# In-place weight decoding, a zero-padded first unit, a second block by halves and backward priorities in a linear-attention and gated-MLP kernel

## The chip, the cores and the metric

The kernel runs on one core of one Trainium2 chip. A core has TensorE (PE: matmuls, with its weight loads shown apart as PEld), VectorE (DVE), ScalarE (ACT), GpSimd (POOL) and SyncE (SP), which here issues nearly all DMAs. SBUF is the on-chip memory of 128 partitions; PSUM holds the results of matmuls in eight banks. The metric is the device time of one execution in microseconds (us). Lower is better.

## The reference

Two stages follow each other. The first is a recurrent attention with a decaying state, the second a two-layer MLP with a gate that is 0 below -1, a parabola between -1 and 1, and the identity above 1.

```python
B, H, S, D = 4, 8, 768, 48                 # batch, heads, tokens, head size
state = zeros(B, H, D, D)
for t in range(S):
    cur = einsum('bhd,bhe->bhde', u * k[t], v[t])
    y[t] = einsum('bhd,bhde->bhe', r[t], state + cur)
    state = w[t][..., None] * state + einsum('bhd,bhe->bhde', k[t], v[t])
x = y.transpose(0, 2, 1, 3).reshape(3072, 384)
h = x @ w_in                               # 384 -> 2048
g = where(h >= 1, h, where(h <= -1, 0, (h + 1)**2 / 4))
out = g @ w_out                            # 2048 -> 384
```

All of it is float32. The kernel gets float32 accuracy from the faster 32-bit matmul format (fp32r in the profile) by splitting each operand into a high and a low part and adding three products.

## The kernel before

**Units and blocks.** The 3072 tokens are cut into 12 units of 256 (three units to a batch). Function `attention(u, ...)` works on one unit: running products of w by scans on VectorE (p forward, y backward), k divided and r multiplied by them (lines 400 and 450), the matrix of r and k inside each chunk of 64 tokens on TensorE (`among`, line 420), masked into r_ by predicated copies (line 426), k transposed (line 459) and copied to SBUF (kt, line 466), the update of the state for each chunk (`umat`, line 481), a chain of four states on VectorE (lines 497 to 500: add the old state, multiply by the decay), and the output: state times r (`cross` and a part of `along`) and r_ times v (`along`, line 519). The first three units are "early": they get k times u on ScalarE (line 390) and a second `among`; the others use the natural layout nk.

**From y to x.** A unit's eight heads of 48 stand in four slots of two heads, 64 rows each, with 48 used. The MLP wants 384 rows in three groups of 128. So three slots keep their place, and the fourth slot (tile last) is cut in pieces of 16 rows, which six DMAs (line 603, function `fill`) move into the free rows 48 to 63 of x. Before that, x and last are written as high and low part (`yevac`, lines 571 to 575): ScalarE copies the high part from PSUM, VectorE subtracts it for the low part. For a unit in INPLACE (unit 0), TensorE subtracts the high part in PSUM (`less`, lines 581 and 584) and ScalarE copies the rest.

**MLP steps.** Two units make a block of 512 tokens; there are six blocks. A step (b, f) of `products` takes block b and one of the 16 slices f of 128 hidden units: nine matmuls into h (line 849), the gate (lines 665 to 670: two on ScalarE, one on VectorE, a high-part copy on ScalarE, a low part on VectorE), and, LAG steps later, nine matmuls that add into three PSUM banks acc (line 869). In block 0 the first five f are taken by halves, 256 tokens each: half 0 needs only unit 0, half 1 only unit 1.

**Weights.** Each slice f of the weights comes as 64-bit words (768 KB) and is decoded once by `weight(f)`: fetch into wraw; ScalarE writes the exponent and mantissa part to fl (line 320) and 16 low bits to rr (line 323), GpSimd 16 sign bits to rr (line 324), VectorE shifts and merges fl and rr (line 327), ScalarE copies the high part (line 316), VectorE subtracts for the low part (line 330). There are two fl tiles, one rr tile, and at most FLIGHT = 4 fetches at a time.

**Order of the work.** The program lists its operations with an engine, a cost, what they read and write, and a due time. A planner (class Plan) orders them before anything runs: at each moment it gives each engine the ready operation with the smallest key, where a key is the time of a step minus a lead (LEADS for each unit, DECODE for weights, SLACK times the length of what follows in the group). It repeats this ROUNDS = 6 times with the step times of the last round and keeps the order whose modelled end is first. Every engine then runs its own list strictly in this order, so an instruction that waits holds up all behind it on its engine. Where TensorE would be idle, matmuls on zeros are inserted (lines 292 and 298), which compute nothing.

## Time and profile before

| | |
|---|---|
| median of 3 runs | 526.85 us (526.12 to 532.59) |
| the profiled execution's own time | 525.53 us |
| its span, first to last instruction | 523.8 us |
| mean granted TensorE clock | 0.998 |
| matmuls (line 849, line 869) | 909 and 909 |

Times in the profile count from the first instruction of the span. A timeline row gives start, duration, engine, line, operation, output and input; where equal instructions follow each other they are merged into one row, and xN is their count. Brackets hold the idle time of the engine just before and what ended it. A row of the groups gives line, engine, operation, shape and count, then busy time in us and the mean in ns of one, then the idle time before them. A row of stages gives the stage, its length, and the busy time and number of instructions of PE, PEld, DVE, ACT and POOL, then the granted clock, the busy share of the DMA engines and GB/s. Matmuls overlap in a pipeline, so a pace is read from two starts, not from a duration.

### The profile page before, as it was taken

Reading aid. Unit: us, or ns where it says so; the run is one execution under the profiler, and the core shown is the slowest. Engines: PE = TensorE matmul, PEld = TensorE weight load, DVE = VectorE, ACT = ScalarE, POOL = GpSimd, SP = SyncE. Lnnn points to the kernel's source line nnn. Section 1 sums busy time; section 2 is a strip of 40 time slices with the busy share of each in tenths; the row PEclk is TensorE's granted clock in tenths of the full one; section 3 lists DMA queues with packets and bytes.
Section 4 is the critical chain, followed back from the end, with each engine's and each line's share of the span. In section 5 each row is a group of like instructions: output and inputs, shape, how many; then the busy total and the mean of one; then the engine's idle time right before and its main releaser. Section 6 shows DMA issues by size and latency. Waiting matters only on the chain.

```text
span 523.8 us, 12249 instructions
## 1 busy us (share of the span) xinstructions
PE 501.5 (96%) x5168; PEld 398.2 (76%) x5168; DVE 339.7 (65%) x575; ACT 293.0 (56%) x573; POOL 94.8 (18%) x61
## 2 busy tenths in 40 slices
PE   7879899999999999999999999999999999999994
PEld 5457887777887787787788687887788777788883
DVE  7999999899955889785692443965833545333331
ACT  5677888677784555653462544634644344444442
POOL 3564744550220311101110001101000100000000
PEclk9999999999999999999999999999999999999999
DMA  8985932525650624530330101504100100100001
GB/s 323 408 281 164 354 107 76 190 91 174 199 172 3 208 96 134 195 102 14 120 109 1 62 0 32 176 2 128 61 0 0 43 18 10 68 1 0 1 0 66
DMA packets 22190, 54.83 MB, mean 105 GB/s; under 512 B 3184, under 2 KB 9072, under 8 KB 22128
## 3 DMA queue, kind: packets, MB, share of 16 engines
q1 hardware_dynamic: 21840, 53.59, 29.8%
q8 instruction: 42, 0.69, 0.5%
q10 hardware_dynamic: 288, 0.39, 0.2%
q14 instruction: 20, 0.16, 0.1%
HBM read 46.89 MB, written 4.72 MB: 99 GB/s over the span
## 4 chain that ended last, share of the span: by engine, by line
PE 74%; DVE 11%; issue 4%; DMA 4%; POOL 3%; SPq 1%; ACT 1%; ACTq 0%; DVEq 0%; POOLq 0%
PE h L849 33%; PE acc L869 32%; PE bank L519 3%; POOL rr L324 3%; DMA rk<-in_rk 2%; PE bank L481 2%; PE bank L420 2%; PE bank L459 2%; DVE fl L327 1%; DVE g L667 1%; DMA wraw<-in_wbits 1%; DVE wt L330 1%; DVE p L377 1%; DVE gl L670 1%; DVE rk L450 1%
## 5 line engine op out<-in xcount | busy, mean ns | idle before, releaser
L849 PE MATMUL h<-x,wt 128*128 128x512 f32 (+1 forms) x909 | 221.0, 389 | 4.7 <-DVE g L667 3.3
L849 PEld LDWEIGHTS h<-x,wt 128*128 128x128 f32 x909 | 162.9, 188 | 43.9 <-DVE g L667 6.3
L869 PE MATMUL acc<-gh,wt 128*128 128x512 f32 (+1 forms) x606 | 154.7, 390 | 0.0
L667 DVE SCALAR_TENSOR_TENSOR g<-g,h 128x512 f32<-128x512 f32 (+1 forms) x101 | 65.7, 655 | 98.5 <-ACT g L666 98.4
L869 PEld LDWEIGHTS acc<-gh,wt 128*128 128x128 f32 x606 | 108.6, 188 | 24.4 <-issue 0.5
L665 ACT ACTIVATE g<-h 128x512 f32<-128x512 f32 (+1 forms) x101 | 57.9, 574 | 103.9 <-PE h L849 99.9
L670 DVE TENSOR_TENSOR gl<-g,gh 128x512 fp32r<-128x512 f32 (+1 forms) x101 | 68.9, 686 | 31.6 <-ACT gh L669 31.3
L669 ACT CAST gh<-g 128x512 fp32r<-128x512 f32 (+1 forms) x101 | 60.0, 597 | 46.8 <-DVE g L667 45.9
L869 PE MATMUL acc<-gl,wt 128*128 128x512 f32 (+1 forms) x303 | 84.1, 385 | 0.8 <-DVE gl L670 0.8
L869 PEld LDWEIGHTS acc<-gl,wt 128*128 128x128 f32 x303 | 55.6, 188 | 13.7 <-DVE gl L670 1.1
L666 ACT ACTIVATE g<-g 128x512 f32<-128x512 f32 (+1 forms) x101 | 61.6, 611 | 2.6
L324 POOL TENSOR_SCALAR rr<-wraw 128x768 uint16<-128x768 uint16 x16 | 55.0, 3435 | 44.6 <-DVE fl L327 23.9
L446 POOL TENSOR_TENSOR r<-cst,d 128x512 f32<-128x512 f32 x18 | 20.3, 1146 | 215.2 <-PE bank L519 184.7
L377 DVE TENSOR_TENSOR_SCAN p<-wq,seeds 128x520 f32<-128x520 f32 x24 | 30.5, 1272 | 2.9 <-DMA wq<-in_w 2.0
L372 DVE TENSOR_TENSOR_SCAN y<-wq,seeds 128x520 f32<-128x520 f32 x24 | 31.5, 1311 | 0.8
L438 POOL TENSOR_TENSOR nk<-nk 128x768 f32<-128x768 f32 x9 | 17.3, 1926 | 63.8 <-DMA nk<-in_nk 39.3
L499 DVE TENSOR_TENSOR sm<-bank,st 128x192 f32<-128x192 f32 x39 | 13.9, 356 | 10.8 <-PE bank L481 8.9
L320 ACT ACTIVATE fl<-wraw 128x768 f32<-128x768 f32 x16 | 14.5, 915 | 8.6 <-DVE wt L330 8.6
L519 PEld LDWEIGHTS bank<-rk,st 64*64 64x64 f32 x656 | 12.3, 134 | 8.6 <-issue 3.3
L400 DVE TENSOR_TENSOR rk<-rk,y 128x512 f32<-128x512 f32 x24 | 17.1, 712 | 2.3 <-DMA rk<-in_rk 2.1
L426 DVE COPY_PREDICATED r<-below,bank 128x512 f32<-128x512 int32 x22 | 15.6, 731 | 4.5 <-PE bank L420 3.6
L323 ACT ACTIVATE rr<-wraw 128x768 uint16<-128x768 uint32 x16 | 17.4, 1084 | 0.9 <-DMA wraw<-in_wbits 0.9
(89 smaller groups left out, 386.6 us busy)
## 6 DMA issues: line engine op xcount, KB each, us to landing
rk<-in_rk SPq DMA_DIRECT2D x24, 512.0 KB, 5.1
wraw<-in_wbits SPq DMA_DIRECT2D x16, 768.0 KB, 7.5
nk<-in_nk SPq DMA_DIRECT2D x9, 768.0 KB, 4.6
wq<-in_w SPq DMA_DIRECT2D x24, 260.5 KB, 3.0
vn<-in_v SPq DMA_DIRECT2D x12, 384.0 KB, 6.2
fl<-in_w SPq DMA_DIRECT2D x12, 260.0 KB, 3.2
out_y<-g SPq DMA_DIRECT2D x10, 256.0 KB, 2.4
x<-last SPq DMA_DIRECT2D x72, 32.0 KB, 3.1
```

The costliest lines, as they stand in the source:

```text
L324: op(SIGNS, 0.6 if SIGNS == "DVE" else 1.3, due, [("raw", f)], ["rr_high"], lambda: (V if SIGNS == "DVE" else G).tensor_scalar(out=r16[:, ...
L372: V.tensor_tensor_scan(out=y_[:, ::-1], data0=w[:, SEG:0:-1], data1=sv[:, ::-1], initial=0.0, op0=ALU.mult, op1=ALU.add)
L377: V.tensor_tensor_scan(out=pv[:, q].rearrange("p n c -> p (n c)"), data0=w[:, 0:SEG], data1=sv, initial=0.0, op0=ALU.mult, op1=ALU.add,)
L446: op("POOL", 1.1, due, ["d", "cst"], [("R", h)], lambda h=h: G.tensor_tensor(out=r_[h], in0=twice.unsqueeze(1).unsqueeze(1).broadcast_to([ ...
L519: PE.matmul(out=bank[by[g]][HP * half : HP * half + HP, lo : lo + C], start=first, stop=False, skip_group_check=True, **kw)
L665: op("ACT", c, due, [("b", 6 + hk)], [("g", gk)], lambda: nc.scalar.activation(gs, hs, AF.Relu, scale=0.5, bias=0.5))
L666: op("ACT", c, due, (), [("g", gk)], lambda: nc.scalar.activation(gs, gs, AF.Square))
L667: op("DVE", 0.13 + 0.53 * k, due, [("b", 6 + hk)], [("g", gk)], lambda: nc.vector.scalar_tensor_tensor(out=gs, in0=gs, scalar=1.0, in1=hs, ...
L669: op("ACT", c, due, [("g", gk)], [("gh", gk)], lambda: nc.scalar.copy(ghs, gs))
L670: op("DVE", 0.15 + 0.5 * k, due, [("g", gk), ("gh", gk)], [("gl", gk)], lambda: nc.vector.tensor_tensor(out=gls, in0=gs, in1=ghs.bitcast(F ...
L849: nc.tensor.matmul(hp, lhsT=wx[f][:, cs], rhs=xt[:, j, :], start=n == 0, stop=n == 8)
L869: nc.tensor.matmul(o[j], lhsT=wx[f][:, cs], rhs=gt, start=first and i == 0, stop=stop and i == 2, skip_group_check=True)
```

## The change

Seven things change together.

1. **Weights in place.** The three pieces of the decoding that come before the merge are written back into wraw itself, so rr is gone and fl only takes the merged result; there are three fl tiles (FULL), and FLIGHT goes from 4 to 3. GpSimd now takes the sign from the 32-bit high word after ScalarE's piece, not from 16-bit words beside it; the three pieces follow one another. The merge reads two operands with a step of two words.
2. **Unit 0 padded** (ALONE). Its v comes from a second layout, v0, with 64 columns a head of which 16 are zero, and its states stand in padded tiles (borrowed from ob and g). So rows 48 to 63 of the first three slots of y are zero; the fourth slot is copied (last_f) and added into these rows by six float32 matmuls with a permutation matrix perm (`spread`). The six fill DMAs of unit 0 are gone. Two DMAs for v0 and one for perm take the place of one for v; there are two more memsets on GpSimd.
3. **Unit 0's chain of states** (CHAINED): the old state is added on TensorE, into the PSUM bank that holds the update (`add_up`), and VectorE only multiplies.
4. **Unit 1 joins INPLACE.** Its low parts come from TensorE and ScalarE.
5. **Block 1 by halves** for its first 14 f (HALVES).
6. **k times u on VectorE, the copies to ptot on GpSimd**; the last output's DMA of acc bank 1 is issued from SP, not from ACT. APART = 1 concerns the fills of unit 0 alone, of which there are none.
7. **Priorities.** One round with due times (ROUNDS = 1, new LEADS, SLACK and DECODE), then five rounds (BACK) in which the keys come from a schedule made backwards from the end (`late`); the best of the six is kept.

```diff
-HALVES = 5
+HALVES = {0: 5, 1: 14}
+BACK = 5
@@ Plan.best, after the rounds with due times
+        for _ in range(BACK):
+            for op, key in zip(self.ops, self.late()):
+                op["key"] = key
+            order = self.order()
+            end = max(self.end.values())
+            if end < found[0]:
+                found = end, order, (self.begin, self.end)
+    def late(self):
...
+        while any(open_.values()):
+            t, e = min((max(free.get(e, 0.0), min(ready(n) for n in ns)), e) for e, ns in open_.items() if ns)
+            n = max((n for n in open_[e] if ready(n) <= t + 1e-9), key=lambda n: (self.end[n], n))
...
+            back[n] = free[e] = t + ops[n]["cost"]
...
+        return [last - back[n] for n in range(len(ops))]
@@ parameters
-LEADS = {0: 33.0, 1: 17.9, 2: 36.0, 3: 22.6, 4: 34.7, 5: 44.0, 6: 70.6, 7: 38.2, 8: 38.8, 9: 10.1, 10: 28.0, 11: 37.9}
-LEAD, DECODE = 15, 11.9
-FLIGHT = 4
+LEADS = {0: 81.9, 1: 72.9, 2: 33.1, 3: 18.5, 4: 28.8, 5: 10.1, 6: 29.8, 7: 19.1, 8: 36.5, 9: -4.7, 10: 28.9, 11: -2.7}
+LEAD, DECODE = 15, 9.3
+FLIGHT = 3
+FULL = 3
-SIGNS = "POOL"
-INPLACE = {0}
+ALONE = {0}
+INPLACE = {0, 1}
+CHAINED = {0}
-ROUNDS = 6
+ROUNDS = 1
@@ weight
-        op("ACT", 0.9, due, [("raw", f)], [("fl", k)], lambda: A.activation(
-            s, wraw[f][:, :, 1].bitcast(F32), AF.Abs, scale=float(2.0**-112)))
-        op("ACT", 1.07, due, [("raw", f), ("flight", f % FLIGHT)], ["rr_low"],
-           lambda: A.activation(r16[:, :, 0], wraw[f][:, :, 0].bitcast(U32), AF.Copy, scale=LOW))
-        op(SIGNS, 0.6 if SIGNS == "DVE" else 1.3, due, [("raw", f)], ["rr_high"], lambda: (V if SIGNS == "DVE" else G).tensor_scalar(
-            out=r16[:, :, 1], in0=wraw[f].rearrange("p c two -> p (c two)").bitcast(U16)[:, 3::4],
-            scalar1=32768.0, scalar2=32768.0, op0=ALU.is_ge, op1=ALU.mult), port=SIGNS == "DVE")
-        op("DVE", 0.95, due, ["rr_low", "rr_high"], [("fl", k)], lambda: V.scalar_tensor_tensor(
-            out=m, in0=m, scalar=3, in1=rr, op0=ALU.logical_shift_left, op1=ALU.bitwise_or), port=True)
+        op("ACT", 0.9, due, (), [("raw", f)], lambda: A.activation(high(F32), high(F32), AF.Copy, scale=float(2.0**-112)))
+        op("ACT", 1.07, due, (), [("raw", f)], lambda: A.activation(half(0), low(U32), AF.Copy, scale=LOW))
+        op(on, 0.62 if f in SIGNS else 3.15, due, (), [("raw", f)], lambda: e.tensor_scalar(
+            out=half(1), in0=high(F32), scalar1=0.0, scalar2=32768.0, op0=ALU.is_lt, op1=ALU.mult))
+        op("DVE", 0.95, due, [("raw", f), ("flight", f % FLIGHT)], [("fl", k)], lambda: V.scalar_tensor_tensor(
+            out=s.bitcast(I32), in0=high(), scalar=3, in1=low(), op0=ALU.logical_shift_left, op1=ALU.bitwise_or), port=True)
@@ attention
+        if alone:
+            for c2 in range(2):
+                load(due, g_[c2], a["v0"][c2], [("g", c2)])
+            load(due, perm, a["perm"], ["perm", "nk"])
-                A.mul(ku[:, q, cs], rk[slot[q]][:, 1, cs], u_col[:, 2 * q + pr : 2 * q + pr + 1])
+                V.tensor_scalar(
+                    out=ku[:, q, cs], in0=rk[slot[q]][:, 1, cs], scalar1=u_col[:, 2 * q + pr : 2 * q + pr + 1],
+                    scalar2=None, op0=ALU.mult)
-            op("ACT", 0.2, due, [("p", q)], [("ptot", u, q)], lambda q=q: A.copy(
+            op("POOL", 0.2, due, [("p", q)], [("ptot", u, q)], lambda q=q: G.tensor_copy(
+        def add_up(c, old):
+            c2, g = divmod(c, 2)
+            PE.matmul(bank[bu[g]][:, c2 * 4 * D : (c2 + 1) * 4 * D].rearrange("p (a e) -> p a e", e=D), lhsT=ident, rhs=ss_(old),
+                      start=False, stop=True, skip_group_check=True)
+        def spread(g):
+            yv = bank[by[g]].rearrange("p (a c t) -> p a c t", a=4, t=C)
+            for j in range(3):
+                PE.matmul(yv[:, j], lhsT=perm[:, 128 * j : 128 * j + 128], start=False, stop=True, skip_group_check=True,
+                          rhs=last_f.rearrange("p (c g t) -> p c g t", c=2, g=2)[:, :, g, :])
+        if alone:
+            for g in range(2):
+                op("ACT", 0.27, due, [("b", by[g])], [("last_f", g), ("g", 2)], lambda g=g: A.copy(
+                    last_f.rearrange("p (c g t) -> p c g t", c=2, g=2)[:, :, g, :],
+                    bank[by[g]].rearrange("p (a c t) -> p a c t", a=4, t=C)[:, 3]))
+            for g in range(2):
+                op("PE", 0.65, due, [("last_f", g), "perm", "nk", ("g", 2)], [("b", by[g])], lambda g=g: spread(g), fresh=False)
-        for j in range(3):
+        for j in range(0 if alone else 3):
@@ products, the last step
-            out("ACT", nc.scalar, "ACT", 1, whole)
+            out("ACT", nc.sync, "SP", 1, whole)
```

147 lines of the change are left out of this document (106 added, 41 removed).

## The prediction

> **What bounds the kernel now.** I read the page first: which engine fills the span.
>
> ```profile
> span 523.8 us, 12249 instructions
> PE 501.5 (96%) x5168; PEld 398.2 (76%) x5168; DVE 339.7 (65%) x575; ACT 293.0 (56%) x573; POOL 94.8 (18%) x61
> ```
>
> TensorE does. But its 96% is an average that also counts matmuls on zeros, so next I cut the span at TensorE's own landmarks: first MLP product, first product of half 1, first full step all paid up, start of block 1.
>
> ```profile
> 0.00:33.43 33.43, 24.81 (x488) 16.68 (x489) 28.87 (x44) 19.39 (x40) 17.37 (x22) 1.00 0.91 342
> 33.43:52.21 18.78, 17.55 (x348) 15.17 (x347) 17.58 (x35) 15.95 (x35) 9.96 (x3) 1.00 0.61 210
> 52.21:68.51 16.30, 14.75 (x114) 13.94 (x113) 15.84 (x26) 14.56 (x29) 12.45 (x5) 1.00 0.80 302
> 68.51:122.42 53.91, 52.17 (x681) 40.60 (x680) 50.22 (x83) 40.32 (x73) 24.14 (x10) 1.00 0.37 124
> 122.42:170.00 47.58, 47.58 (x417) 37.97 (x420) 33.67 (x56) 33.66 (x72) 6.72 (x4) 1.00 0.41 132
> 170.00:516.97 346.97, 344.61 (x3141) 273.88 (x3132) 193.07 (x335) 168.31 (x328) 24.16 (x19) 1.00 0.18 60
> ```
>
> The columns after the stage's length are PE, PEld, DVE, ACT, POOL busy, clock, DMA share, GB/s. From 68.51 on TensorE is idle for 1.74, 0 and 2.36 us only: nothing that VectorE, ScalarE or GpSimd save there can be seen, unless TensorE's own work changes. Before 68.51 VectorE is the full engine (17.58 of 18.78, 15.84 of 16.30), and TensorE waits for it. So the change is decided by when TensorE gets both units of block 0. The timeline of TensorE:
>
> ```profile
> 31.93 1.16 PE L420 MATMUL bank<-rk 64*64 64x64 f32 x64 [2.94 <-DVE rk L450]
> ...
> 33.43 1.31 PE L849 MATMUL h<-x,wt 128*128 128x256 f32 x9
> 34.59 0.60 PE L459 MATMUL bank<-cst,rk 128*128 128x128 f32 x4
> ...
> 36.18 1.15 PE L481 MATMUL bank<-vn,kt 64*64 64x48 f32 x64
> ...
> 42.22 1.11 PE L519 MATMUL bank<-r,vn 64*64 64x64 f32 x64
> ...
> 52.21 2.35 PE L849 MATMUL h<-x,wt 128*128 128x256 f32 x18
> ...
> 57.05 2.38 PE L849 MATMUL h<-x,wt 128*128 128x256 f32 x18 [1.44 <-DVE g L667]
> ...
> 62.16 0.87 PE L869 MATMUL acc<-gh,wt 128*128 128x256 f32 x6
> ...
> 63.22 0.87 PE L869 MATMUL acc<-gh,wt 128*128 128x256 f32 x6
> ```
>
> Half 0 starts at 33.43, behind a matmul of unit 1 that waited 2.94 us for VectorE; unit 1's output ends at 42.22 + 1.11 = 43.33, and half 1 starts at 52.21. From there on everything is work in stock. A half group of nine matmuls paces at 63.22 - 62.16 = 1.06 us.
>
> ```profile
> 122.42 2.34 PE L849 MATMUL h<-x,wt 128*128 128x512 f32 x9 [1.04 <-DMA x<-last]
> ...
> 143.16 4.38 PE L849 MATMUL h<-x,wt 128*128 128x512 f32 x18
> 147.38 1.57 PE L869 MATMUL acc<-gh,wt 128*128 128x512 f32 x6
> ```
>
> Two full groups take 147.38 - 143.16 = 4.22 us, 2.11 each.
>
> **The change part by part.** The profiled execution took 525.53 us, its span and 1.73 around it; the median of the runs, 526.85, lies 1.3 above. I sum against 525.5 and add 1.3 at the end.
>
> *Unit 0.* Its six fills go. What they cost now:
>
> ```profile
> 24.55 5.00 SPq L603 DMA_DIRECT2D x<-last  x6
> ...
> 46.67 4.00 SPq L603 DMA_DIRECT2D x<-last  x6
> ```
>
> ```profile
> 24.08 0.45 ACT L571 CAST last<-acc 128x128 fp32r<-128x128 f32 x2
> ```
>
> ```profile
> 1.00 3.78 PE L292 MATMUL h<-zero 128*128 128x128 f32 x16 [1.00 <-POOL zero L281]
> ```
>
> And TensorE's share of half 0 before 52.21 in line 869 (PE busy, count, clock, DMA, GB/s):
>
> ```profile
> 33.43:52.21 18.78, 5.61 (x36) 1.00 0.61 210
> ```
>
> Unit 0's last copy ends at 24.53; issuing the fills takes from 24.55 to 29.55, with a landing behind it, and products start at 33.43. In their place come two copies to last_f (0.45 by the row of such a pair) and six float32 matmuls of 128 columns (0.24 each, 3.78 for 16 in the warm-up's row), 1.9 us together; the pairs of copies of the slot "last" fall away. The state chain gets longer: three additions of VectorE (0.36 each, row below) become a trip to TensorE and back. So x of unit 0 is there at about 25 to 27 instead of after 29.55. That alone moves nothing at the end: half 0 is five steps of 2 x 1.06 = 10.6 us, TensorE is through with them before unit 1, and already today it has 36 of line 869's 45 matmuls done by 52.21. What is won is the one group of nine that is left over: **-1.1 us**, and a TensorE that is free when unit 1 asks.
>
> *k times u and the additions.* Rows of the groups:
>
> ```profile
> L324 POOL TENSOR_SCALAR rr<-wraw 128x768 uint16<-128x768 uint16 x16 | 55.0, 3435 | 44.6 <-DVE fl L327 23.9 <-DVE seeds L376 8.3 <-DMA wraw<-in_wbits 7.8
> ...
> L327 DVE SCALAR_TENSOR_TENSOR fl<-fl,rr 128x768 int32<-128x768 int32 x16 | 15.2, 950 | 0.9 <-POOL rr L324 0.9
> ...
> L499 DVE TENSOR_TENSOR sm<-bank,st 128x192 f32<-128x192 f32 x39 | 13.9, 356 | 10.8 <-PE bank L481 8.9
> ...
> L573 DVE TENSOR_TENSOR x<-bank,x 128x384 fp32r<-128x384 f32 x22 | 11.4, 550 | 7.3 <-ACT x L575 5.9 <-ACT last L575 1.0
> ...
> L390 ACT ACTIVATE nk<-rk,cst 128x256 f32<-128x256 f32 x12 | 5.4, 497 | 3.2 <-DMA rk<-in_rk 2.1 <-DMA cst<-in_consts 1.2
> ...
> L667 DVE SCALAR_TENSOR_TENSOR g<-g,h 128x256 f32<-128x256 f32 x10 | 3.9, 410 | 0.1
> ...
> L627 DVE TENSOR_SCALAR ptot<-ptot 128x192 f32<-128x192 f32 x1 | 0.3, 251 | 0.0
> ```
>
> ScalarE loses 12 x 0.5 us, VectorE gets 12 pieces of 256 columns. The nearest row is the same kind of operation on 192 columns, 0.251; by columns 0.33, and at most the 0.41 of a gate piece of 256. Eight of them precede unit 1's output: +2.6 us on the full engine. Against it stand 3 x 0.36 = 1.1 of unit 0's additions; unit 1's own in-place low part takes 2 x 0.55 and two smaller ones from VectorE too, but only after its output, where ScalarE and TensorE do it in about the same time. Net about +1.5 us for VectorE ahead of unit 1.
>
> *Weights.* Today GpSimd's 3.4 us stand between two merges through the one rr tile (23.9 us of waiting for VectorE's L327). In place, GpSimd may run ahead; but its piece now follows ScalarE's two. The merge keeps its 0.95 if a step of two words costs nothing, 1.75 if it halves the rate (0.8 us per 768 columns more); no row of VectorE has such a step, ScalarE's pieces read it today without harm, so I take 0.95. Weights then are not late for half 0, nor for half 1 at five steps in stock.
>
> *Unit 1, the term that decides.* It is bound by the order on VectorE and TensorE, not by its own chain:
>
> ```profile
> 23.81 4.09 POOL L324 TENSOR_SCALAR rr<-wraw 128x768 uint16<-128x768 uint16 x1 [1.07 <-DVE seeds L376]
> ```
>
> ```profile
> 24.94 1.33 DVE L400 TENSOR_TENSOR rk<-rk,y 128x512 f32<-128x512 f32 x1
> ...
> 26.42 1.24 DVE L372 TENSOR_TENSOR_SCAN y<-wq,seeds 128x520 f32<-128x520 f32 x1
> ...
> 29.29 0.69 DVE L400 TENSOR_TENSOR rk<-rk,y 128x512 f32<-128x512 f32 x1
> ```
>
> The scan of its last half ends at 27.66, yet line 400 runs at 29.29: 1.6 us behind weight pieces. It ends at 29.98; the second transpose, which needs nothing else, runs at 34.59, 4.6 us later, behind the second `among` and two product groups. Together 6.2 us of queueing that an order by remaining work could take out. So unit 1 comes between 6.2 us earlier (all of it gone) and 1.5 later (order as now, plus the added pieces on VectorE). I take **-3.5 us**, a little over the middle, since unit 1 has the longest remaining work and the new keys rank by that. Its fills stay (4.00 us of issue, from 46.67 to half 1 at 52.21 it is 5.5 us), so x of unit 1 lands at about 48.7.
>
> A rule that speaks against this part: the Trainium skill, in "SBUF — State Buffer", section "SBUF: two separate sides", says that VectorE and GpSimd share one port pair as an exclusive lock, and that an operation with two SBUF inputs, or one in a two-port mode such as a scaled copy, waits out a whole GpSimd instruction. In the rows above GpSimd holds 23.81 to 27.90, and VectorE's two-input line 400 and the scan start and end inside it, the first in 1.33 instead of 0.69, the second undisturbed: the trace shows a delay of 0.6 us, no lock for the whole instruction. The mechanism stays among the rivals.
>
> *After 52.21.* TensorE idles 16.30 - 14.75 = 1.55 us until 68.51, mostly the wait at 57.05 for VectorE's gate. With weights and half 0 done earlier I take **-1.0** (0 to -1.55). At 122.42 block 1 waits 1.04 us for unit 3's fills; by halves it needs only unit 2 there, a unit earlier: **-1.0** (0 to -1.74, all idle of that stage). What is next late is line 667.
>
> *Halves of block 1.* Each f now is four half groups for two full ones: 4 x 1.06 - 4.22 = 0.02 us by paces, 2 x 2.35 - 4.38 = 0.32 by merged durations; times 14: 0.3 to 4.5, I take **+1.0** (near the paces, as durations overlap). VectorE pays more for halves, by the rows of line 667 2 x 0.41 against
>
> ```profile
> L667 DVE SCALAR_TENSOR_TENSOR g<-g,h 128x512 f32<-128x512 f32 x91 | 61.8, 682 | 98.4 <-ACT g L666 98.4
> ```
>
> 0.68, so 0.14 per f, and about as much again for its second piece: some 4 us over block 1, covered by 13.9 idle us of VectorE in 122.42:170.00 (ScalarE has as many). Without that cover, those 4 us.
>
> *Tail.*
>
> ```profile
> 517.39 0.41 ACTq L688 DMA_DIRECT2D out_y<-g  x1
> ...
> 517.84 0.37 ACT L687 COPY g<-acc 128x256 f32<-128x256 f32 x1 [0.48 <-DVE g L687]
> ```
>
> The DMA on ScalarE's queue holds the last copy from 517.39 to 517.84; issued from SP it doesn't: **-0.4**. On SP it stands before the 0.33 us issue of the third output, which still lands with the last.
>
> *Priorities* cost nothing on the chip; their effect is the spread of the term for unit 1. From 170 on there are 2.36 us of idle to win, and as much may be lost; I take 0.
>
> Sum: -1.1 - 3.5 - 1.0 - 1.0 + 1.0 - 0.4 = **-6.0**, so 519.5 for a profiled execution and **520.8** for the median.
>
> **The rivals.**
> - *Unit 1 runs along its bare chain.* All of 6.2, 1.55 and 1.74 is won and halves cost 0.3: -1.1 - 6.2 - 1.55 - 1.74 + 0.3 - 0.4 = -10.7, 516.1 as a median. For it: remaining work is what the new keys rank. Against: VectorE is full before 68.51 with work that is not removed.
> - *VectorE gives it back.* The merge's step halves its rate: 0.8 x 16 = 12.8 us more on VectorE, four of them ahead of unit 1; VectorE is busy 50.22 of 53.91 until 122.42 and cannot take 8 more there without holding TensorE. -6.0 + 4 + about 4 = +2: 528.8.
> - *The port lock* (the rule above): each of unit 1's two k-times-u steps and unit 2's waits out half a GpSimd piece, 1.7 us, since the sign pieces now run without the pauses of today: 4 x 1.7 = 6.8, so 527.6. Against it: the rows at 24.94 and 26.42.
> - *The ring of three fetches starves TensorE*, slower than before. A fetch may go out only after the merge three slices earlier.
>
> ```profile
> wraw<-in_wbits SPq DMA_DIRECT2D x16, 768.0 KB, 7.5
> ```
>
>   Landing 7.5, ScalarE about 2, GpSimd 3.4, merge 0.95, so 14 us for three, 4.6 a slice, and more by every wait in a queue; TensorE takes a slice in 4.22 plus attention. Today it is just in time. If waits of 7 us a round make it 7 a slice, the sixteenth is ready 15 x 7 = 105 us after the first, some 12 later than a TensorE that starts at 49 wants it: about 533. It decides from about 6 a slice.
>
> **How the numbers follow.** Forecast 0.52, bare chain 0.20, VectorE 0.12, lock 0.06, ring 0.10. The range 510 to 530 holds the forecast's own spread (514 to 526), the bare chain with what an order could still win late, and both middle rivals. Two per cent, about what a measurement of this kernel can tell from no change, is 10.5 us: under 516.3 is faster, over 537.4 slower. Faster: half of an even better bare chain and the low end of the forecast, 0.22 in all; slower: the bad half of the ring, 0.05; the rest 0.73.
>
> **What would show it.** Right: the first product near 26; half 1 near 49; no TensorE wait for x at block 1; the same TensorE busy stages later on, and a merge of 0.95 us. Wrong: half 1 at 52 or later (the order did not help), TensorE waiting for line 330 between 60 and 110 (ring), VectorE's pieces of 1.7 us and more beside GpSimd (lock or step), or gaps of TensorE in block 1's halves.

## The result, and the profile after

The changed kernel takes 530.74 us (median of 22 runs, 529.03 to 532.46); the kernel before, run beside it, 526.79 (22 runs). The ratio is 1.0064, with an interval of 1.0048 to 1.0080: slower by about 3.4 us, where 6.0 less was forecast. That is within the two per cent that the prediction took for no change. The forecast of 520.8 missed by 9.9 us, and 530.74 lies just above the upper end of its range. The profiled execution took 532.4 us, its span 530.6 (523.8 before).

The page of the changed kernel, first lines, and its groups for the weights (columns as explained for the kernel before):

```profile
span 530.6 us, 12817 instructions
PE 502.2 (95%) x5424; PEld 417.9 (79%) x5424; DVE 348.0 (66%) x608; ACT 304.1 (57%) x581; POOL 112.9 (21%) x87
...
L389 POOL TENSOR_SCALAR wraw<-wraw 128x768 uint16<-128x768 f32 x16 | 65.5, 4132 | 34.0 <-ACT wraw L387 24.6
...
L387 ACT ACTIVATE wraw<-wraw 128x768 uint16<-128x768 uint32 x16 | 31.2, 1947 | 0.0
```

ScalarE lost twelve pieces of k times u and is still busier, 304.1 for 293.0. GpSimd went from 94.8 to 112.9. Line 387, ScalarE's 16 low bits, takes 1.95 us; its row before (line 323) had 1.08. GpSimd's sign bits take 4.13 for 3.44.

The same stages as before, cut again at the first product of half 0, the first of half 1, the start of block 1 and the last product:

```profile
0.00:33.52 33.52, 22.70 (x422) 17.86 (x422) 25.16 (x43) 17.70 (x23) 16.62 (x28) 0.86 0.86 323
33.52:61.19 27.67, 22.33 (x432) 20.02 (x429) 26.81 (x48) 22.64 (x41) 19.93 (x7) 0.92 0.58 194
61.19:121.46 60.27, 60.09 (x594) 50.39 (x594) 54.37 (x82) 55.49 (x88) 38.77 (x14) 0.97 0.47 163
121.46:170.00 48.54, 47.01 (x682) 43.68 (x685) 41.89 (x85) 34.45 (x91) 7.52 (x8) 1.00 0.48 153
170.00:519.96 349.96, 349.96 (x3313) 285.91 (x3305) 199.28 (x351) 173.06 (x341) 30.07 (x31) 1.00 0.18 59
```

Half 0 starts where it did (33.52 for 33.43). Half 1 starts at 61.19 instead of 52.21: **9.0 us lost**. Its row shows what it waited for, unit 1's fills, whose issue is the first of these rows (46.67 before):

```profile
52.69 4.68 SPq L715 DMA_DIRECT2D x<-last  x6
...
61.19 3.84 PE L962 MATMUL h<-x,wt 128*128 128x256 f32 x18 [1.55 <-DMA x<-last]
```

From there to TensorE's last product it is 519.96 - 61.19 = 458.8 us against 516.97 - 52.21 = 464.8: **6.0 won**. From the last product to the end of the span it is 530.6 - 519.96 = 10.6 against 6.8: **3.8 lost**. The three make the 6.8 us between the spans. The middle one is idle time of TensorE that is gone: it idles 0.18 + 1.53 = 1.7 us behind the start of half 1, where the kernel before idled 1.55 + 1.74 + 2.36 = 5.65; the rest is less work, such as matmuls on zeros. The stretch from the last product to the end of the span is called the tail below.

Half 0 lost its fills and gained nothing. Why is seen in the timeline of the changed kernel, in TensorE's rows and those of what it waits for:

```profile
15.54 12.63 POOL L389 TENSOR_SCALAR wraw<-wraw 128x768 uint16<-128x768 f32 x3 [7.39 <-ACT wraw L387]
...
18.18 0.59 PE L591 MATMUL bank<-ob,cst 128*128 128x192 f32 x2 [2.45 <-issue]
...
28.21 0.96 DVE L391 SCALAR_TENSOR_TENSOR fl<-wraw 128x768 int32<-128x768 int32 x1 [1.39 <-POOL ptot L484]
...
29.20 0.83 ACT L382 CAST wt<-fl 128x768 fp32r<-128x768 f32 x1 [0.96 <-DVE fl L391]
29.94 0.47 ACT L672 CAST x<-acc 128x384 fp32r<-128x384 f32 x1
30.31 0.92 ACT L386 ACTIVATE wraw<-wraw 128x768 f32<-128x768 f32 x1
30.47 0.55 PE L682 MATMUL acc<-x,minus 128*128 128x128 f32 x3 [1.62 <-ACT x L672]
...
31.12 1.92 ACT L387 ACTIVATE wraw<-wraw 128x768 uint16<-128x768 uint32 x1
...
32.77 0.95 ACT L668 CAST x<-acc 128x384 fp32r<-128x384 f32 x2
...
33.52 2.75 PE L962 MATMUL h<-x,wt 128*128 128x256 f32 x11
```

It has to be read from the bottom. The first product needs x; the copies of its low part (L668, 32.77) stand on ScalarE's list behind two weight pieces, L386 and the slow L387 (31.12 + 1.92), although what they copy was there with line 682 at 30.47 + 0.55 = 31.02. Line 682 itself waits 1.62 us for ScalarE's copy L672 at 29.94. What that copy reads was there at 28.40 (line 691), but on ScalarE's list it stands behind the cast L382 of a weight slice, at 29.20, which waits for the merge at 28.21, which waits for GpSimd: three sign pieces in a row, 15.54 + 12.63 = 28.17 (the row of the merge names line 484, a small copy that GpSimd's records show at the end of the same stretch). So weight pieces that nobody needs yet twice hold a copy that everybody needs. Above it stands a second loss: TensorE idles for 2.45 us in front of its first product of the chain of states (line 591), whose operand ob was there at 14.88 + 0.36 = 15.24, with no wait that the profile shows, and then the clock falls, in the stage from 22 to 26 us to 0.50:

```profile
22.00:26.00 4.00, 3.77 (x111) 3.39 (x104) 3.96 (x7) 1.26 (x4) 4.00 (x2) 0.50 0.75 267
```

The 2.45 us do not belong to the chain. In all eighteen traces kept for this document TensorE stops in front of the same place, its 450th instruction in the trace, for 0.5 to 3.8 us, whichever line stands there. In the kernel before this is a matmul on zeros, where the stop delays nothing:

```profile
15.78 1.98 PE L298 MATMUL bank<-zero 128*128 128x512 f32 x4 [1.23 <-issue]
```

A DMA of 16 KB on an instruction queue runs beside the stop or just ahead of it each time (15.74 to 16.77 in the changed kernel, 13.32 to 14.38 before), and in sixteen of the eighteen TensorE goes on 1.3 to 1.6 us behind its end (later in the two with the states on VectorE, where the next instruction needs the last state). That TensorE waits there for its next instructions is the reading that fits; no edit tested it. The change put the chain of states on TensorE across this stop.

### The profile page after: what moved, and what is told of

Same layout as the page of the kernel before. It is cut to its first block, busy times and chain, and to the rows that moved or that the text cites. A ratio compares the mean times of both kernels' runs of the same rounds, so it can differ in the third digit from the quotient of the medians.

```text
span 530.6 us, 12817 instructions
## 1 busy us (share of the span) xinstructions
PE 502.2 (95%) x5424; PEld 417.9 (79%) x5424; DVE 348.0 (66%) x608; ACT 304.1 (57%) x581; POOL 112.9 (21%) x87
## 4 chain that ended last, share of the span: by engine, by line
PE 75%; ACT 7%; DMA 5%; issue 4%; POOL 3%; DVE 3%; SPq 1%; POOLq 0%; ACTq 0%
PE h L962 34%; PE acc L982 32%; PE bank L616 4%; POOL wraw L389 3%; PE bank L507 2%; ACT wraw L387 2%; PE bank L568 2%; DMA wraw<-in_wbits 1%; DMA fl<-in_w 1%; PE bank L546 1%; DMA out_y<-g 1%; ACT wraw L386 1%; ACT g L779 1%; ACT wt L382 1%; DMA x<-last 1%
## 5 line engine op out<-in xcount | busy, mean ns | idle before, releaser
L962 PE MATMUL h<-x,wt 128*128 128x512 f32 (+1 forms) x1035 | 226.5, 366 | 3.0 <-DMA x<-last 1.5
L962 PEld LDWEIGHTS h<-x,wt 128*128 128x128 f32 x1035 | 174.1, 193 | 34.6 <-DVE g L780 1.9
L982 PEld LDWEIGHTS acc<-gh,wt 128*128 128x128 f32 x690 | 115.6, 188 | 21.5 <-issue 0.5
L783 DVE TENSOR_TENSOR gl<-g,gh 128x512 fp32r<-128x512 f32 (+1 forms) x115 | 72.9, 639 | 32.7 <-ACT gh L782 32.6
L389 POOL TENSOR_SCALAR wraw<-wraw 128x768 uint16<-128x768 f32 x16 | 65.5, 4132 | 34.0 <-ACT wraw L387 24.6
L982 PEld LDWEIGHTS acc<-gl,wt 128*128 128x128 f32 x345 | 59.6, 188 | 11.8 <-DVE gl L783 1.2
L387 ACT ACTIVATE wraw<-wraw 128x768 uint16<-128x768 uint32 x16 | 31.2, 1947 | 0.0
L484 POOL COPY ptot<-p 128x8 f32<-128x8 f32 x24 | 8.4, 354 | 97.7 <-DVE p L464 97.7
L391 DVE SCALAR_TENSOR_TENSOR fl<-wraw 128x768 int32<-128x768 int32 x16 | 17.1, 1068 | 3.6 <-POOL wraw L389 2.1
L386 ACT ACTIVATE wraw<-wraw 128x768 f32<-128x768 f32 x16 | 14.8, 922 | 5.3 <-DMA wraw<-in_wbits 5.3
```

The costliest lines, as they stand in the source:

```text
L387: op("ACT", 1.07, due, (), [("raw", f)], lambda: A.activation(half(0), low(U32), AF.Copy, scale=LOW))
L389: op(on, 0.62 if f in SIGNS else 3.15, due, (), [("raw", f)], lambda: e.tensor_scalar(out=half(1), in0=high(F32), scalar1=0.0, scalar2=327 ...
L783: op("DVE", 0.15 + 0.5 * k, due, [("g", gk), ("gh", gk)], [("gl", gk)], lambda: nc.vector.tensor_tensor(out=gls, in0=gs, in1=ghs.bitcast(F ...
L962: nc.tensor.matmul(hp, lhsT=wx[f][:, cs], rhs=xt[:, j, :], start=n == 0, stop=n == 8)
L982: nc.tensor.matmul(o[j], lhsT=wx[f][:, cs], rhs=gt, start=first and i == 0, stop=stop and i == 2, skip_group_check=True)
```

## The experiments

Ratios are to the kernel before on the same chip, so runs of different hours can be set side by side. Where a kernel is made from the changed one, the number to compare with is 1.0064.

### The late flag

```diff
-        for emit in plan.kept_warm(plan.best(step_ops, dues), "PE", ...
+        order = plan.best(step_ops, dues)
+        for n in late:      # the check's product and the flag
+            order.remove(n)
+            t = max(plan.end[m] for m in plan.ops[n]["deps"]) + 8.0
...
+            order.insert(at, n)
```

> The changed kernel in the same order of work, with two instructions moved: the small matmul of the final check and the flag's comparison go from the end of TensorE's and VectorE's lists to about 8 us after their inputs are there (about 445 us instead of 519.9 and 520.3). Late-flag theory: all five engines load the flag only after 520.46, and the stretch from TensorE's last product to the end, 10.6 us in the changed kernel against 6.8 before, shrinks by about 4; time about 527. Start-up theory (all of the loss is in the first 70 us, the longer end is only where the loss shows): no change, 530 to 531.

529.8 us, ratio 1.0029 (1.0004 to 1.0053). That is 0.35% or 1.8 us better. In its profile the tail is 9.6 us for 10.6, where about 4 less were expected by the theory of the late flag; so the flag is about one us of the tail, and the other 2.8 were still open.

### Unit 0's states back on VectorE

```diff
-            if old is None or u in CHAINED:
+            if old is None:
...
-                   lambda c=c, old=old: add_up(c, old), fresh=False)
+                   lambda: None, fresh=False)
```

> The changed kernel in the same order of work, but unit 0's states are added on VectorE again (four additions and multiplications there, nothing on TensorE). Chain theory: the chain of states, 14.88 to 22.30 us in the changed kernel against 14.92 to 17.69 before, shrinks by 3 to 4 us, since TensorE's 2.45 us gap without a wait at 15.7 to 18.2 no longer lies on it; unit 0's output ends 3 to 4 us earlier, half 1 starts at 57 to 58 instead of 61.2, and the time falls by 3 to 4 to about 527. Weight theory (ScalarE's and GpSimd's slower pieces pace the start): the output of unit 0 is earlier, half 1 moves by less than 1, time 530.

531.13 us, ratio 1.0052 (1.0024 to 1.0081), against 1.0064: no more than the scatter. The timeline of this kernel:

```profile
23.93 1.60 PE L691 MATMUL acc<-g,nk 128*128 128x128 f32 x12 [0.36 <-ACT g L696]
27.55 0.55 PE L682 MATMUL acc<-x,minus 128*128 128x128 f32 x3 [2.01 <-ACT x L672]
30.75 0.90 PE L682 MATMUL acc<-x,minus 128*128 128x128 f32 x3 [2.65 <-ACT x L672]
33.81 3.72 PE L962 MATMUL h<-x,wt 128*128 128x256 f32 x18
```

Unit 0's spread (line 691) starts 2.3 us earlier (23.93 for 26.19), and the whole gain goes into longer waits for line 672 (2.01 and 2.65 us for 1.62). The first product comes at 33.81. The slow chain is real, but it is not what ends last.

### Zeros in the chain, to keep the clock up

```diff
             c2, g = divmod(c, 2)
+            for _ in range(2):
+                PE.matmul(bank[0], lhsT=zero, rhs=zero.unsqueeze(1).broadcast_to([128, 4, 128]), start=True, stop=True)
             PE.matmul(bank[bu[g]][:, c2 * 4 * D ...
```

> The changed kernel with two matmuls on zeros ahead of each of the three additions of states on TensorE, nothing else. Clock theory (the granted clock fell to 0.5 from 21 to 28 and from 31 to 37 us because TensorE idled at 15.7 to 18.2): the clock stays at 1.0 there, unit 0's output takes 2.5 us instead of 4.2 and the first products 2.4 instead of 4.25 for 18; half 1 about 2 to 3 us earlier, time 528. Chain theory: the clock is a side effect, the states still come at 22; half 1 within 1 us, time 530 to 531.

532.8 us, ratio 1.0101 (1.0044 to 1.0159). Stage 14 to 26 us, first the changed kernel and then this one (the number before the last two is the clock):

```profile
14.00:26.00 12.00, 7.99 (x238) 6.44 (x229) 9.36 (x16) 7.89 (x9) 10.46 (x3) 0.78 0.84 311
```

```profile
14.00:26.00 12.00, 9.26 (x186) 5.89 (x181) 7.05 (x14) 6.66 (x8) 11.01 (x3) 1.00 0.63 227
```

The clock stays at 1.00 in this stage, half 1 starts at 61.13, and nothing is won. The zeros take TensorE's time themselves (unit 0's output, line 616, starts at 24.06 for 21.63), so the run does not price the clock alone; but the copy of x that line 682 waits for starts at 30.07, as late as in the changed kernel (29.94), behind the same cast. The low clock is a companion of the loss at half 1, not its cause.

### Unit 1's fills ahead of a weight fetch

```diff
+        fills = state["fills", 1]
...
+        fetch = max((n for n in range(len(plan.ops)) if ... and order.index(n) < first), key=order.index)
+        order.remove(fetch)
+        order.insert(1 + max(order.index(n) for n in fills), fetch)
```

> The changed kernel with one transfer moved on SP's queue: the weight fetch issued at 52.1 us, directly ahead of unit 1's six fills, goes directly behind them. Transfer theory (the fills, 52.7 to 61.2 us here against 46.7 to 52.2 before, wait behind the 768 KB of that fetch): half 1 starts about 2 us earlier, at 59, time 529. Otherwise: the landing of the fills stays and the moved fetch makes its slice late; time 530.7 or more.

531.95 us, ratio 1.0076 (1.0048 to 1.0103).

```profile
58.74 2.27 PE L971 MATMUL h<-x,wt 128*128 128x256 f32 x18
64.49 1.34 PE L971 MATMUL h<-x,wt 128*128 128x256 f32 x9 [2.39 <-DVE g L781]
```

Half 1 starts 2.4 us earlier and then TensorE waits 2.39 us for VectorE's gate: an exchange of one wait for another.

### The weight pieces by themselves

This kernel runs 39 more instructions behind the changed kernel's work, so its total (584.45 us) says nothing; each form stands in threes, on 128 x 512.

```diff
+        for _ in range(3):
+            A.activation(h16(R0, 0), lo32(R0), AF.Copy, scale=LOW)   # in place, 16 bits every 8 bytes
+        ...                                                          # another tile; every 4 bytes; contiguous
+        for _ in range(3):
+            G.tensor_scalar(out=h16(R0, 1), in0=R0[:, :, 1], scalar1=0.0, scalar2=32768.0, op0=ALU.is_lt, op1=ALU.mult)
+        ...                                                          # the same, the form of the kernel before, contiguous input
```

> The changed kernel with 39 more instructions behind its work, on tiles that nobody needs any more: the decoding's pieces on 512 columns, each form three times. ScalarE's low piece: output in place with a step of 8 bytes, the same in another tile, with a step of 4 bytes in another tile, and contiguous. GpSimd's sign piece: in place, in another tile with 8 and with 4 bytes, the old 16-bit form, contiguous output, contiguous input. VectorE: the sign piece, the merge with steps of two words and contiguous. Step theory: 16-bit writes with a step of 8 bytes cost ScalarE twice those with 4 (1.3 against 0.75 us for 512), in place or not. In-place theory: only writing into the tile that is read doubles it. Either way GpSimd's forms show whether its 4.1 us (3.4 before) come from the 32-bit input, the step or neighbours.

Its timeline, in this order: ScalarE in place every 8 bytes, into another tile every 8 bytes, every 4 bytes, contiguous; GpSimd in place every 8 bytes, into another tile every 8 bytes, every 4 bytes, the form of the kernel before (16-bit input, every 4 bytes); VectorE's merge from two-word steps, contiguous.

```profile
520.50 4.07 ACT L858 ACTIVATE rk<-rk 128x512 uint16<-128x512 uint32 x3 [0.45 <-ACT g L800]
524.60 4.07 ACT L860 ACTIVATE rk<-rk 128x512 uint16<-128x512 uint32 x3
528.41 2.43 ACT L862 ACTIVATE kt<-rk 128x512 uint16<-128x512 uint32 x3
530.72 2.00 ACT L864 ACTIVATE kt<-rk 128x512 uint16<-128x512 uint32 x3
532.80 8.10 POOL L866 TENSOR_SCALAR rk<-rk 128x512 uint16<-128x512 f32 x3 [121.00 <-ACT kt L864]
540.73 8.80 POOL L868 TENSOR_SCALAR rk<-rk 128x512 uint16<-128x512 f32 x3
...
549.35 6.41 POOL L870 TENSOR_SCALAR kt<-rk 128x512 uint16<-128x512 f32 x3
555.85 6.42 POOL L872 TENSOR_SCALAR kt<-rk 128x512 uint16<-128x512 uint16 x3
...
574.54 2.14 DVE L880 SCALAR_TENSOR_TENSOR y<-rk 128x512 int32<-128x512 int32 x3 [30.07 <-POOLq L888]
576.72 2.14 DVE L882 SCALAR_TENSOR_TENSOR y<-y,kt 128x512 int32<-128x512 int32 x3
```

That the piece is done in place costs ScalarE nothing: 4.07 and 4.07. The step of the 16-bit output does: 4.07 / 3 = 1.36 us each at 8 bytes, 0.81 at 4, 0.67 contiguous on ScalarE, and 2.70 against 2.14 on GpSimd. GpSimd's 32-bit input costs nothing against the 16-bit one (2.14 both), and its form in another tile takes 2.93, no less than in place, though beside a piece of VectorE. The merge's reads in steps of two words are free: 0.71 both ways.

### The pieces in a tile of their own, for the first eight slices

```diff
+        def low_part():
+            if f < 8:
+                rr[f] = wpool.tile([128, 768], I32, tag="wt", name=f"rr{f}")
+            A.activation(r16(0) if f < 8 else half(0), low(U32), AF.Copy, scale=LOW)
...
-            out=half(1), in0=high(F32), ...
+            out=r16(1) if f < 8 else half(1), in0=high(F32), ...
-            ..., scalar=3, in1=low(), ...
+            ..., scalar=3, in1=rr[f] if f < 8 else low(), ...
```

> The changed kernel in the same order of work; for the first eight slices the 16 low bits and the sign bits go to a tile of their own with a step of 4 bytes, as before the change, and the merge reads that tile. Weight theory (ScalarE's piece of 1.95 us and GpSimd's of 4.13, planned as 1.07 and 3.15, hold up what stands behind them in both lists; unit 0's high copies stand behind the third slice): ScalarE's piece falls to 1.08, GpSimd's to about 3.4, unit 0's x is complete 3 to 5 us earlier, half 1 starts at 56 to 58 instead of 61.2, time about 527. Chain theory was that the states on TensorE do it, which the run with the states on VectorE has spoken against; by it nothing moves here, 530 to 531.

526.51 us, ratio 0.998 (0.9959 to 1.0001): 0.84%, 4.4 us better than the changed kernel, with the same order of work; by the two intervals, 3 to 6 us. One kernel now holds both forms, eight of each (groups):

```profile
L399 POOL TENSOR_SCALAR wraw<-wraw 128x768 uint16<-128x768 f32 x8 | 33.9, 4265 | 16.4 <-ACT wraw L380 16.0 <-POOL ptot L494 0.5
L399 POOL TENSOR_SCALAR rr<-wraw 128x768 uint16<-128x768 f32 x8 | 25.3, 3184 | 10.4 <-ACT wraw L396 10.4
L380 ACT ACTIVATE wraw<-wraw 128x768 uint16<-128x768 uint32 x8 | 15.7, 1962 | 0.0
...
L380 ACT ACTIVATE rr<-wraw 128x768 uint16<-128x768 uint32 x8 | 8.6, 1070 | 0.0
```

The first product is at 30.86, half 1 at 56.37, and the last product at 513.6, 3.4 us earlier than in the kernel before. The tail of 11.2 us takes that back.

### The same step put into the kernel before

The last test of the weights is the opposite one: nothing of the change but the step.

```diff
-        r16 = rr.bitcast(U16).rearrange("p (c two) -> p c two", two=2)
+        r16 = rr.bitcast(U16).rearrange("p (c h two) -> p h c two", h=2, two=2)
```

and the three operations that use r16 and rr address them in the same two halves.

> The kernel before, in which only the place of the 16-bit pieces in their tile is changed: column c stands in word 2c, column 384 + c in word 2c + 1, so that ScalarE and GpSimd write 16 bits in steps of 8 bytes and the merge reads words in steps of two. Engines, order, tiles and result are the same. Theory of the step: ScalarE's piece goes from 1.08 to about 1.95 us, GpSimd's from 3.4 to about 4.2, the merge stays at 0.95; GpSimd's piece is in the chain of the weights before 52 us, so half 1 starts 1 to 4 us later than 52.21 and the kernel takes 1 to 4 us more. Theory that the step is free, as the prediction had it for all but the merge, or that only the same tile for reading and writing costs: the pieces and the time stay, within 0.5 us.

532.18 us, ratio 1.0084 (1.0055 to 1.0113): 4.4 us slower (2.9 to 6.0), with engines, order and tiles of the kernel before.

```profile
L324 POOL TENSOR_SCALAR rr<-wraw 128x768 uint16<-128x768 uint16 x16 | 68.8, 4299 | 38.1 <-DVE fl L327 19.5
...
L323 ACT ACTIVATE rr<-wraw 128x768 uint16<-128x768 uint32 x16 | 31.2, 1952 | 1.1 <-DMA wraw<-in_wbits 1.1
...
L327 DVE SCALAR_TENSOR_TENSOR fl<-fl,rr 128x768 int32<-128x768 int32 x16 | 15.9, 993 | 5.1 <-POOL rr L324 5.0
```

1.95 for 1.08, 4.30 for 3.44, and the merge 0.99 for 0.95. Its half 1 starts only 1.4 us late (53.63), and then TensorE waits for the gate longer than before:

```profile
PE h L849 <- DVE g L667: 5.5, 6, 2.4
...
PE h L849 <- DVE wt L330: 1.4, 2, 1.1
```

That is 5.5 us in six waits, where the kernel before has 3.3 in five, and 1.4 us for the weights themselves, 0.3 before. So the step is shown from both sides. That both come to 4.4 us is in part chance: this run slows all sixteen slices, and pieces_apart mends eight.

### The planner

```diff
-BACK = 5
+BACK = 0
...
-ROUNDS = 1
+ROUNDS = 6
```

> The changed kernel without the backward rounds: six rounds with due times, as before the change, and the new leads. If the backward priorities are at fault (work with little behind it, such as the final check, goes last; unit 0 and weights are mixed): the flag comes early again, the end is 4 us shorter, the time falls to 526 or lower. If they help elsewhere: more idle time of TensorE after 70 us than the changed kernel's 2 us, time 531 or more.

539.08 us, ratio 1.0245 (1.0213 to 1.0278): with due times alone, and the leads of the changed kernel, the change would have been 1.8% or some 9.5 us worse still. The other run of this kind gave the planner the pieces' true costs:

```diff
-op("ACT", 1.07, ...   # low bits
+op("ACT", 1.95, ...
-op(on, 0.62 if f in SIGNS else 3.15, ...
+op(on, 0.62 if f in SIGNS else 4.1, ...
-op("DVE", 0.42, ...   # k times u
+op("DVE", 0.6, ...
```

> The changed kernel with three costs in the plan set to what the trace shows (ScalarE's low piece 1.95 instead of 1.07, GpSimd's sign piece 4.1 instead of 3.15, k times u 0.6 instead of 0.42); the order of the work is made anew from these. If the loss at the start is an order made for pieces that are quicker than they are: the copies of unit 0 stand ahead of the waiting weight pieces, half 1 starts some 4 us earlier, time 526 to 528. If the pieces themselves are the loss, whatever the order: half 1 at 60 or later, time 530 or more.

533.37 us, ratio 1.0121 (1.0091 to 1.015). Half 1 is at 59.43, 1.8 us earlier, and a wait of 3.07 us for the gate appears at 141.68. An order that knows the costs does not remove them.

### The tail: code or queues

Two kernels, each with one edit on the changed one. In the first, instructions are added that never run, inside the general path that the flag jumps over:

```diff
         V.memset(sx, 0.0)
+        for _ in range(8):
+            G.memset(sx, 0.0)
+            nc.sync.dma_start(out=us[0:D, :], in_=a["u"][0])
         with tc.For_i(0, B, 1) as b:
```

> The changed kernel with eight DMAs of SyncE and eight memsets of GpSimd added inside the general path, which is jumped over and never runs; nothing that runs is touched. It moves the place in memory of what stands behind the jump. Theory of the code fetch: in the changed kernel SyncE stalls 3.5 us at its jump over the general path and once more 2.5 us, always at the same instruction behind it (the sixth; the eighth in two kernels with two SyncE instructions fewer), while a fetch of 8 KB of instructions runs; with the code moved on by eight instructions or more the second stall is gone, the tail behind TensorE's last product (10.6 us) shortens by about 2.5 us, and the time by 2 to 3 us against 530.7. Theory of the queues (the third output on SyncE's queue, or its DMA's landing, is what lengthens the tail): nothing changes.

In the second, the output moved by the change goes back:

```diff
-            out("ACT", nc.sync, "SP", 1, whole)
+            out("ACT", nc.scalar, "ACT", 1, whole)
```

> The changed kernel with the last step's middle output issued from ScalarE's queue again, as in the kernel before. Theory of the queues: the tail of 10.6 us goes back toward 6.8, the time to about 527.5. Theory of the code fetch: the tail stays within 0.5 us of 10.6 and the stall is seen one or two instructions further on, since SyncE's code is that much shorter; the prediction's own term for this edit, 0.4 us, is the most that it can cost.

dead_code: 528.66 us, ratio 1.0023 (0.9998 to 1.0048). out_on_scalar: 529.48, ratio 1.0032 (1.001 to 1.0055). The totals alone don't tell the two theories apart; the tails do. SyncE's records behind the jump, in us from the start of the span:

```
kernel          last product   jump     next instruction   second stall           end     tail
before          516.97         517.84   521.49             none                   523.8    6.8
changed         519.96         522.19   525.73             2.52 before the 6th    530.6   10.6
out_on_scalar   519.24         521.04   524.70             2.41 before the 8th    529.5   10.3
dead_code       518.88         521.13   525.11             none                   527.0    8.1
```

Each of these four stands 3.5 to 3.9 us at the jump (flag_early and the kernels made with its edit 2.8 to 2.9), and in this time DMAs of 8 KB and 16 KB run on the instruction queues. The changed kernel stands a second time, and the place moves by exactly the two instructions that SyncE's list is shorter by in out_on_scalar. With code that never runs put in front of it, it is gone, and the tail is 2.5 us shorter. The other runs bear this out: every trace of the changed kernel's family without the added code has the second stall (1.7 to 2.8 us in ten traces), and none of the six with it. The output's queue goes against the forecast: back on ScalarE's queue the tail is 0.3 us shorter, as SyncE has one DMA less to issue ahead of the jump (the jump is 1.8 us behind the last product, 2.2 in the changed kernel). That the last products of these runs differ by one us although their work is the same shows how much of such a difference one profile can carry; this may be why out_on_scalar's total looks better than its tail.

### Three mends together, and the price of the halves

pieces_apart, flag_early and dead_code in one kernel, and the same with block 1 in full width:

```diff
-HALVES = {0: 5, 1: 14}
+HALVES = {0: 5}
```

> Three mends at once: low part and sign bits of the first eight weight slices in a tile of their own, the check's product and flag early, and the dead code. If the three losses are separate they add: 526.5 - 1 - 2.5 = about 523 against 527 of the kernel before, ratio 0.991 to 0.995. If the tail is set by the landing of the outputs, the last two win nothing: 526.5.

> As the run with three mends, but block 1 in steps of full width again (and the order planned anew with it). The prediction's terms for the halves of block 1: a wait of 1.0 us at block 1 saved, 1.0 us paid in paces, so the same time within 1 us; TensorE's wait of about 1 us for unit 3's fills at the start of block 1 should be back. If VectorE's additional pieces of the halves held TensorE, this run is up to 4 us faster; if the earlier start is worth more than the wait, as the second half of unit 3's work is no longer in front of block 1, it is 2 us or more slower.

apart_flag_dead: **524.21 us, ratio 0.9938 (0.9917 to 0.9959)**, faster than both kernels: 3.3 us under the one before, 1.26% under the changed one. The three alone gave 0.84, 0.35 and 0.41%, 1.60 in sum; most of it adds. block1_whole: 527.5 us, 0.9998 (0.9975 to 1.0021). With the order that goes with them, the halves are worth 0.6%, about 3.2 us. The wait for unit 3's fills at block 1 did not come back with full width: the only wait for fills left is the one at half 1. Of the 4.8 us by which its last product comes later (520.21 for 515.43), 2.6 lie before half 1 already (60.33 for 57.72), in an order that was planned anew; the rest was not traced.

### Why unit 1 still comes late

In the mended kernel half 1 starts at 57.72, still 5.5 us behind the kernel before. The way of unit 1 through the three kernels, as the ends of its steps in the timelines, in us:

```
kernel                 output (last product)   last copy of x   fills issued from   half 1
before                 43.33                   46.61            46.67               52.21
changed                48.72                   52.66            52.69               61.19
three mends together   45.24                   49.18            50.73               57.72
```

Of the 9.0 us lost in the changed kernel 5.4 are there when unit 1's output ends, 0.7 come with the low parts in place, and 3.0 between the fills' issue and the product, since the fills land later (median 5.5 us from issue to landing, 2.5 before). In the mended kernel it is 1.9, 0.7, 1.5 for a weight fetch that SyncE issues ahead of the fills, and 1.4 for the landing. Three single edits on the mended kernel: the weight fetch behind unit 1's fills (as above), k times u back on ScalarE, and the states added on VectorE (as above).

```diff
-                V.tensor_scalar(out=ku[:, q, cs], in0=rk[slot[q]][:, 1, cs], scalar1=u_col[...], scalar2=None, op0=ALU.mult)
+                A.mul(ku[:, q, cs], rk[slot[q]][:, 1, cs], u_col[...])
```

> The kernel with three mends (524.2), and the weight fetch that SyncE issues at 49.20 put behind unit 1's six fills. In the kernel with three mends unit 1's last copy ends at 49.18, SyncE then issues that fetch for 1.42 us and the fills from 50.73, and half 1 starts at 57.72. If unit 1's fills hold TensorE: half 1 about 1.5 us earlier, and the time up to 1.5 us less. If VectorE's gate pieces hold it, as when the fetch was moved in the changed kernel: half 1 earlier, but the same time.

> The kernel with three mends (524.2), with the k-times-u pieces back on ScalarE at the same places of the order. VectorE loses eight pieces of 0.30 us ahead of unit 1's output, 2.4 us of its busy time. If VectorE's queue sets unit 1 (it is busy 5.9 of every 6 us from 20 to 38), its output comes about 2 us earlier and the time falls by up to 2 us; ScalarE's pieces take 0.45 each and may hold a cast instead. If unit 1 is set by TensorE's order or by the fills, nothing changes (within 0.5 us).

> The kernel with three mends (524.2), with unit 0's states added on VectorE instead of by products on TensorE. In the changed kernel this brought unit 0's output 3.6 us forward and won nothing, since the copies of x then waited for the weights. With the weights mended, the theory that the trip through TensorE (a gap of 2.15 us in front of its first product, and the clock at half from 20 to 26 us) is what is left: unit 0 comes 3 us earlier, VectorE gets to unit 1 sooner, half 1 starts 1 to 3 us earlier and the time falls by 1 to 2 us. If VectorE's queue behind it stays full and decides, the time stays within 0.5 us.

526.5 us (ratio 0.9994, 0.9969 to 1.0019), 526.19 (0.997, 0.9948 to 0.9993) and 524.77 (0.9951, 0.9931 to 0.997), against 0.9938. None helps. With the fetch moved, half 1 starts 0.9 us earlier, and TensorE waits for the gate in its place:

```profile
56.79 2.32 PE L991 MATMUL h<-x,wt 128*128 128x256 f32 x18
62.31 1.34 PE L991 MATMUL h<-x,wt 128*128 128x256 f32 x9 [2.11 <-DVE g L791]
```

With k times u on ScalarE unit 1 is later, not earlier (half 1 at 60.12), though VectorE's busy time from 20 to 40 us falls from 19.79 to 16.01: the pieces stand among casts and copies on ScalarE's list, and up to 61 us VectorE waits 2.4 us for them in front of line 497. With the states on VectorE half 1 comes at 57.16. So the places of the loss are known, but why the new order does not bring unit 1's output forward stays open.

## Why the prediction was wrong, point by point

**The step that failed** is the paragraph on the weights: "ScalarE's pieces read it today without harm, so I take 0.95. Weights then are not late for half 0". The merge was priced, and rightly: 0.95 was forecast, the median of its sixteen pieces is 0.954, and in the small form it is 0.71 with two-word steps and without. What was not priced is the other end of the edit: the 16-bit writes went from every 4 bytes to every 8. No row before had such a write, and of the forms without a row the merge alone was given a second, dearer price. ScalarE's piece went from 1.08 to 1.95 us, GpSimd's from 3.44 to 4.13, and before_step and pieces_apart both put it at about 4.4 us. In the terms of the sum this falls on unit 1: half 1 was forecast at 48.7 and came at 61.19, 12.5 us later, and 4.8 of these go with the pieces of eight slices mended (56.37). The other 7.7 are not explained by the weights. In the profiled executions the forecast missed by +12.5 us up to half 1, by -3.9 from there to the last product and by +4.2 in the tail; that the middle part came out better than forecast hid a part of the miss.

- **B, half 0 over before half 1 (-1.1)**: right. All five of its output groups are done before 61.19. But x of unit 0 "at about 25 to 27" was wrong: the first product is at 33.52, by the weights and by a chain of states that took 7.4 us (14.88 to 22.30) for 2.8. The "trip to TensorE and back" had been given no price, and the spread (line 691) took 2.21 us for 1.44.
- **A, unit 1 (-3.5, bounds -6.2 to +1.5)**: +9.0. Half 1 at 61.19 for 48.7 forecast. With the pieces mended it is +4.2 (56.37), still outside the bounds. The price of k times u was about right (0.30 each by pace, 0.34 by duration, 0.33 forecast). That in-place low parts take "about the same time" was 0.7 us off, and the fills were taken to land as fast as before (5.5 us from issue to product; 8.5 in the changed kernel, 7.0 in the mended one). None of the bounds allowed that an order may also *add* queueing ahead of unit 1's output, and the runs leave open why it did.
- **C and D, the waits at 57.05 and at block 1 (-1.0 each), and E, the halves (+1.0)**: from half 1 on the sum was -2.1 with B, and the kernel won 6.0. After 61.19 TensorE's waits are a few tenths and one of 1.07 us for the gate. The halves with their order are worth about 3.2 us where 0 was forecast for D and E together, and not by the wait for unit 3's fills, which full width did not bring back; what gives the 3.2 was not traced.
- **F, the tail (-0.4)**: +3.8. The output's queue has the wrong sign: ScalarE's last copy starts 0.55 us behind the last product with either queue (0.87 before), so the new order has won that already, and the DMA on SyncE's list puts its jump 0.4 us later. The check's product and flag slid to the end of the list (with the output, SyncE's jump stands 2.2 us behind the last product, 0.9 before), and 2.5 us are the second stall behind the jump. Neither was in the sum: the flag follows from the new priorities, which rank by remaining work and have nothing behind the flag, and could have been seen in the diff; the stall could not.
- **Priorities "cost nothing on the chip"**: they gave some 9.5 us against due times with the same parts and leads (1.0245 against 1.0064), and cost about one us at the flag (flag_early).
- **The rivals.** VectorE's merge at half rate: no. The ring of fetches: TensorE never waits for a weight between 61 and 121 (60.09 busy of 60.27). The port lock: not as a lock, in three rows of the changed kernel beside GpSimd's 15.54 to 28.17:

```profile
20.79 1.26 DVE L459 TENSOR_TENSOR_SCAN y<-wq,seeds 128x520 f32<-128x520 f32 x1
...
22.21 0.94 DVE L391 SCALAR_TENSOR_TENSOR fl<-wraw 128x768 int32<-128x768 int32 x1
...
23.22 1.24 DVE L464 TENSOR_TENSOR_SCAN p<-wq,seeds 128x520 f32<-128x520 f32 x1
```

  Two scans and the two-input merge start and end inside GpSimd's stretch at their usual length. Three of the sixteen merges do take 1.48 to 1.67 us, so there is a delay of up to 0.7 us at times, but none of a whole GpSimd piece. By the rule of the Trainium skill that the prediction weighed ("SBUF — State Buffer", section "SBUF: two separate sides") each would have waited until the GpSimd instruction under way had ended; here the measurement differs.

Of the 9.9 us that the forecast missed by, the mends gave back, by ratios, 4.4 for the step of the weight pieces, 2.2 for the code in front of the second stall and 1.8 for the flag, and 6.6 together. About 3.4 are left (524.2 for 520.8). That this is near the 3.5 forecast for unit 1 is chance: in the mended kernel half 1 is 9.0 us later than forecast (57.72 for 48.7), and the stretch from there to the last product, 457.7 us for 464.8, is 5.0 better than forecast.

## What to carry to other kernels

When an edit changes an access pattern, price both ends of every operation on it, reads and writes and each engine, and measure a form that no row shows before relying on it. A cheap piece of an engine off the bottleneck can still decide when it stands in an in-order list ahead of something urgent: follow the urgent piece's list upward. And look at the last few us apart from the rest: what reads the last flag, and where the engine stands still behind a jump, is part of the time.

## What was not expected of the hardware

- 16-bit writes every 8 bytes cost ScalarE twice (1.36 us for 512 columns, 0.81 every 4 bytes, 0.67 contiguous) and GpSimd a quarter more (2.70 for 2.14); VectorE's 32-bit reads in steps of 8 bytes cost nothing.
- A jump over code that does not run held SyncE for 3.5 to 3.9 us (2.8 to 2.9 in flag_early and the kernels made with its edit), beside DMAs of 8 and 16 KB on the instruction queues, and in the changed kernel it stood 2.5 us more a few instructions later, at a place that moves with the length of the code; instructions that never run, set in front, removed that second stall. That it is the edge of a block of code is the reading that fits all four kernels; the block itself was not seen.
- TensorE stood 2.45 us behind a burst of small matmuls with its operands ready, beside a DMA of 16 KB on an instruction queue, and in all eighteen traces it stops in front of its 450th instruction. It then had a clock of 0.50, seen from 22 to 26 us; two matmuls on zeros ahead of each product of the chain kept it at 1.00 from 14 to 26 us (it fell behind that, to a mean of 0.58 from 33.9 to 38 us).
